# Opening of a chunked-attention and two-MLP kernel: planned with shared DMA time, block 1's attention right behind block 0's, sixteen weight halves' low parts summed on TensorE

## Chip, cores and metric

One core of a Trainium2 chip. The metric is the device time of one execution in microseconds (us), the median of several runs; a profile of one execution shows where it goes.

## What is computed

```python
# q, k, v: 8 x 8 heads x 576 x 64 float32; attention within chunks of 64
scores = scale * np.matmul(q_c, k_c.transpose(0, 1, 2, 4, 3))
scores = scores - np.max(scores, axis=-1, keepdims=True)
attn = np.exp(scores)
attn = attn / (np.sum(attn, axis=-1, keepdims=True) + 1e-09)
out = np.matmul(attn, v_c)
x = out.transpose(0, 2, 1, 3).reshape(4608, 512)
h = x @ w_in                                  # 512 x 2048, float64 weights
g = np.maximum(h, 0.0) + np.log1p(np.exp(-np.abs(h)))
x2 = (g @ w_out).astype(np.float32)           # 2048 x 512
h2 = np.maximum(np.maximum(x2 @ w1, x2 @ w2), x2 @ w3)   # 512 x 768 each
result = (h2 @ w_out2).astype(np.float32)     # 768 x 512
```

## The kernel before

The 4608 tokens are cut into nine blocks of 512 (`NB`). For each block four attention tiles (two heads each) give x in four buffers, then the first MLP runs over 16 column groups j of the hidden size (`NJ`): `mlp1` computes one group's h (`do_h`, line 712, 12 matmuls of 512 columns into a bank `ph`), ScalarE its softplus, ScalarE and VectorE cut g into a high and a low part, and `do_o` (line 732, 12 matmuls) adds into the accumulator `acc`. Each product is made of three passes over high and low parts (`PASS`) in the format fp32r. The second MLP (lines 880 and 990) follows for all blocks.

Blocks 0 and 1 share the opening. Their order is the list `turns`: block 0 for j 0 to 5, block 1 for j 0 to 8, block 0 for j 6 to 15, block 1 for j 9 to 15; a block whose turn ends early copies its accumulator out to memory and adds it again later. Their eight attention tiles (`attention_first`) use TensorE in plain float32: transposes of k and q (line 495), scores (`do_s`, line 526), a softmax on VectorE and ScalarE, a transpose of it (line 486), the product with v (`do_v`, line 575), and a cut into high and low part (`to_x`). Block 0's tiles take any PSUM buffer; block 1's take only `aps`, of which there is one, and come due in the middle of block 0's first turn.

Each of the 32 weight halves (`conv1`: w_in and w_out of each j) comes from memory as raw float64 (512 KB); VectorE makes of it a float32 value `a` and a rest `t` in six instructions (lines 292 to 320), an engine rounds the high part from `a`, and two more VectorE instructions, in `cut_up`, form the low part (`a` minus the high part, plus the rest; line 251). Lines 244, 246 and 251 are helpers that record all copies and two-operand operations.

The order of instructions on each engine is made ahead of time by a planner (`Plan.order`): a list schedule with due times, costs and latencies written by hand, and buffers given out as it goes. On the chip each engine then runs its list in order and waits on semaphores. DMAs are issued by SyncE (SP), and for the first two blocks by ScalarE too; a DMA waits in its engine's list until the DMA eight before it in the program has landed.

Of the kernel before, what the change touches and what calls it, by code (L numbers as in the profile page):

```python
# [20 lines left out]
P = 128  # L21
# [32 lines left out]
class Op:  # L54
    __slots__ = ("engs", "fn", "deps", "allocs", "bufs", "due", "n", "start", "end", "eng", "lat", "succ", "left", "ready", "follow")


class Plan:
# [6 lines left out]
    def op(self, engs, fn, r=(), w=(), alloc=(), hold=(), after=(), due=None, lat=0.0):  # L65
        o = Op()
        o.follow = o.start = None
        o.engs, o.fn, o.due, o.lat, o.allocs = engs, fn, due, lat, list(alloc)
        deps = dict.fromkeys(after)
        bufs = dict.fromkeys(o.allocs + list(hold))  # L70
        for item in r:
            b, key = item if isinstance(item, tuple) else (item, None)
            deps.update(dict.fromkeys(b.writers[key] if key in b.writers and key is not None else sum(b.writers.values(), [])))
            bufs[b] = None
        for item in w:
            b, key = item if isinstance(item, tuple) else (item, None)
            if key is None:
                deps.update(dict.fromkeys(sum(b.writers.values(), []) + sum(b.readers.values(), [])))
            else:
                deps.update(dict.fromkeys(b.writers.get(key, []) + b.readers.get(key, []) + b.readers.get(None, [])))  # L80
            bufs[b] = None
        for item in r:
            b, key = item if isinstance(item, tuple) else (item, None)
            b.readers.setdefault(key, []).append(o)
        for item in w:
            b, key = item if isinstance(item, tuple) else (item, None)
            b.writers[key] = [o]
        for b in bufs:
            if b.first is None:
                b.first = o  # L90
            else:
                deps[b.first] = None
        o.deps = list(deps)
        o.bufs = list(bufs)
        for b in o.bufs:
            b.uses += 1
        o.n = len(self.ops)
        self.ops.append(o)
        return o

    def order(self):
# [13 lines left out]
        now, done = 0.0, []  # L115
        while len(done) < len(ops):
            taken = []
            virt = dict(engine)
            for o in waiting:
# [26 lines left out]
                o.end = engine[best] + o.lat  # L146
                running.append(o)
# [26 lines left out]
def tile_kernel(ctx: ExitStack, tc: tile.TileContext, q, k, v, w_in, w_out, w1, w2, w3, wo2, out):  # L174
# [82 lines left out]
    turns = [(0, 0, 6), (1, 0, 9), (0, 6, NJ), (1, 9, NJ)]  # L257
# [13 lines left out]
    def conv(src, view, kinds, due=None, after=(), most=("load",)):  # L271
# [4 lines left out]
        def load(e):  # L276
# [8 lines left out]
        in_line("load", op({"S": 0.5}, load, w=[raw], alloc=[free, raw], after=after, lat=4.0))  # L285
# [34 lines left out]
            lambda e: nc.vector.scalar_tensor_tensor(t.t, lw().bitcast(U32), 2.0**-52, t.t, ALU.mult, ALU.mult),  # L320
            r=[raw],
            w=[t],
# [15 lines left out]

    def parts_of(z, *keys):
# [61 lines left out]
    def loads(fns, buf, key, alloc=(), engs="S", after=()):  # L401
        for n, fn in enumerate(fns):
            op(
                {e: 0.48 for e in engs},
                lambda e, fn=fn: fn((nc.scalar if e == "A" else nc.sync).dma_start),
                w=[(buf, (key, n))],
                alloc=alloc if n == 0 else (),
                after=after,
                lat=2.2,
            )  # L410
# [9 lines left out]

    def flat(z):
        return z.t if z.place[0] == "ph" else z.t[:, 0]
# [35 lines left out]
    def attention_first(t, after=()):  # L458
# [14 lines left out]
        slow = 1.7  # L473
# [3 lines left out]
        loads(load_plain(t, q, rq), bq, "q", allocs[0], "SA", after)  # L477
        loads(load_plain(t, k, rk), bk, "k", allocs[1], "SA", after)
        loads(load_v(t, rv), bv, "v", allocs[2], "SA", after)
# [22 lines left out]
        op({"P": 0.44 * slow}, turn_in(pk, rk), r=reads(bk, "k"), w=[pk], alloc=[pk])  # L502
# [8 lines left out]
        op({"P": 0.44 * slow}, turn_in(pq, rq), r=reads(bq, "q"), w=[pq], alloc=[pq])  # L511
# [11 lines left out]
        def do_s(e):  # L523
# [11 lines left out]
            {"P": 1.75 * slow},  # L535
# [24 lines left out]
        o = op({"P": 0.44 * slow}, turn(pp, lambda h: pbuf.t[:, h * P:(h + 1) * P]), r=[pbuf], w=[pp], alloc=[pp], due=due_p)  # L560
# [11 lines left out]
        def do_v(e):  # L572
# [11 lines left out]
            {"P": 1.75 * slow},  # L584
# [8 lines left out]
    def attention(t):  # L593
# [5 lines left out]
        loads(load_32(t, q, lambda: Rq.t), Rq, "q", [Rq])  # L599
        loads(load_32(t, k, lambda: Rk.t), Rk, "k", [Rk])  # L600
        loads(load_v(t, lambda: Rv.t), Rv, "v", [Rv])
# [101 lines left out]
    def mlp1(b, j, first, last):  # L703
# [44 lines left out]
        for m in range(KD) if last else ():  # L748
# [14 lines left out]
            else:  # L763
                copy_op(lambda o=o: o.t, src, [acc[m // 2]], [o], psum=True, alloc=[o], due=T0 + STEP * (s + 4))
            store[b, m] = op(
                {"S": 0.48}, lambda e, o=o, m=m, to=to: nc.sync.dma_start(out=to[b][:, m, :], in_=o.t), r=[o], lat=2.5
# [13 lines left out]
    def early(n, due, after):  # L780

        if n < NJ2:
            a, t, _ = conv(wo2, ("out", n), ("x",), after=after)
            z = slot("x")
            cut_up(z, lambda: a.t, [a], alloc=[z], rest=t, due=due)
            store["o", n] = op({"S": 0.48}, lambda e: nc.sync.dma_start(out=wo2d[n], in_=z.t.bitcast(F32)), r=[z], lat=3.0)
# [4 lines left out]
        store["w", n] = op({"S": 0.48}, lambda e: nc.sync.dma_start(out=w2d[n], in_=a.t), r=[a], lat=2.5)  # L791

    def weights2(n):
# [4 lines left out]
        for h, z in enumerate((a, b)):  # L798
# [6 lines left out]
                lat=2.5,  # L805
# [14 lines left out]
    def split(b, after):  # L820
        names = ("B11", "T1", "T2", "B21", "T3", "T4", "B22")
        raw = [slot("x", "z", dt=F32) for _ in range(2)]
        for h in range(2):
# [6 lines left out]
                lat=4.0,  # L830
# [139 lines left out]
    def mlp2_out(b, j):  # L970
# [9 lines left out]
                lat=3.5,  # L980
# [59 lines left out]
    op({"G": 1.0}, lambda e: make_identity(nc, ident), due=-10.0)  # L1040
# [5 lines left out]
    for t in range(HP):  # L1046
        attention_first(t)
    for j in range(NJ):
        c0 = T0 + STEP * (min(place[b, j] for b in range(2)) - 1.5)
        conv1(("a", j, 0), w_in, ("in", j), c0)  # L1050
        done = conv1(("a", j, 1), w_out, ("out", j), c0 + 0.5 * STEP)
        for t in range(HP, 2 * HP) if j == 1 else ():
            attention_first(t, [line["load"]])
    store_early = []
    for n, (b, j, first, last) in enumerate(steps):
        if n >= NJ and n % (NJ // HP) == 0:
            t = HP + n // (NJ // HP)
            if t < NTILE:
# [3 lines left out]
                attention(t)  # L1062
# [46 lines left out]
```

## Time and profile before

| | us |
|---|---|
| median of 3 runs | 1579.29 (1577.02 to 1582.55) |
| the profiled execution | 1575.96 |
| its span, first to last instruction | 1573.8 |
| TensorE busy in it | 1516.1 (96%) |
| VectorE busy | 969.7 (62%) |
| ScalarE busy | 584.5 (37%) |

The profiled execution's own time is 2.2 us above its span. Shares of busy time are averages over stages that differ: the opening, with attention, weight conversion and first loads, and the long rest, in which TensorE alone works without a pause. "The join" is used below for the moment when TensorE starts the first `do_h` of block 1: from then on both blocks have all their attention behind them.

### The profile page before, as it was taken

To read this page: it belongs to the slowest core of one execution; us is meant where nothing else is said; L and a number is where in the kernel's file an instruction comes from. 1 tells how busy PE (TensorE), PEld (TensorE's weight loads), DVE (VectorE), ACT (ScalarE), POOL (GpSimd) and SP (SyncE) were. 2 spreads that over 40 slices of the span, in tenths; PEclk is the share of its full clock that TensorE was granted. 3 is DMA by queue.
4 is the path that set the end of the run, shared out by engine and by line. 5 is a ranking of instruction groups with operands and counts; after the bars stand their busy time and mean duration, and the time that the engine had idled before them with its cause. 6 is when DMAs were issued, how large, how long until landed. Compare 5 with 4: busy or idle time off the path is not lost.

```text
span 1573.8 us, 22841 instructions
## 1 busy us (share of the span) xinstructions
PE 1516.1 (96%) x8866; PEld 1315.8 (84%) x8866; DVE 969.7 (62%) x1859; ACT 584.5 (37%) x1111; POOL 11.9 (1%) x19
## 2 busy tenths in 40 slices
PE   5687999999999999999999999999999999999998
PEld 4566888788888888888888888999999999999997
DVE  4798887786776676776857455544544535445443
ACT  3554244443433434334343343433323323223222
POOL 2000010000000000000000000000000000000000
PEclk8798999999999999999999999999999999999999
DMA  9423314453433434335333121222213223222221
GB/s 248 120 81 103 105 40 112 123 132 98 121 97 75 117 86 108 81 72 132 84 96 102 61 95 54 68 81 81 85 63 108 81 68 108 80 82 73 76 81 67
DMA packets 235211, 147.26 MB, mean 94 GB/s; under 512 B 167008, under 2 KB 202848, under 8 KB 235104
## 3 DMA queue, kind: packets, MB, share of 16 engines
q1 hardware_dynamic: 230544, 143.58, 32.2%
q10 hardware_dynamic: 4560, 2.23, 0.6%
q8 instruction: 69, 1.13, 0.3%
q14 instruction: 38, 0.31, 0.1%
HBM read 109.58 MB, written 36.18 MB: 93 GB/s over the span
## 4 chain that ended last, share of the span: by engine, by line
PE 90%; DVE 4%; DMA 2%; ACT 1%; SPq 1%; issue 1%; ACTq 0%; DVEq 0%
PE acc L732 25%; PE ph L712 25%; PE ph L880 12%; PE aps L880 12%; PE acc L990 10%; DVE tmp L251 3%; PE aps L689 3%; PE aps L636 2%; PE aps L575 1%; ACT s L244 1%; DMA s<-in_v_dram 1%; DMA s<-in_k_dram 1%; PE aps L495 1%; DVE s L251 1%; DMA s<-in_q_dram 0%
## 5 line engine op out<-in xcount | busy, mean ns | idle before, releaser
L732 PE MATMUL acc<-g,s 128*128 128x512 f32 x1728 | 429.1, 397 | 2.3 <-DVE g L251 2.3
L712 PE MATMUL ph<-s,s 128*128 128x512 f32 x1728 | 419.0, 392 | 0.9 <-DVE s L251 0.8
L732 PEld LDWEIGHTS acc<-g,s 128*128 128x128 f32 x1728 | 322.7, 188 | 78.2 <-DVE g L251 2.8
L712 PEld LDWEIGHTS ph<-s,s 128*128 128x128 f32 x1728 | 321.9, 188 | 72.2 <-DVE s L251 1.7
L251 DVE TENSOR_TENSOR tmp<-aps,tmp 128x256 f32<-128x256 f32 x241 | 99.3, 422 | 280.6 <-PE aps L880 217.4
L880 PE MATMUL ph<-s,s 128*128 128x256 f32 x1944 | 267.5, 282 | 0.0
L880 PEld LDWEIGHTS ph<-s,s 128*128 128x128 f32 x1944 | 251.6, 191 | 4.4
L244 ACT COPY tmp<-ph 128x256 f32<-128x256 f32 x268 | 99.8, 372 | 352.9 <-PE ph L880 350.9
L251 DVE TENSOR_TENSOR g<-tmp,g 128x512 fp32r<-128x512 f32 x198 | 134.1, 688 | 134.9 <-ACT g L244 133.5
L880 PE MATMUL aps<-s,s 128*128 128x256 f32 x1458 | 203.7, 285 | 3.6
L722 ACT ACTIVATE tmp<-ph 128x512 f32<-128x512 f32 x144 | 86.3, 599 | 302.9 <-PE ph L712 300.7
L880 PEld LDWEIGHTS aps<-s,s 128*128 128x128 f32 x1458 | 186.1, 191 | 9.0 <-DVE tmp L251 8.6
L990 PE MATMUL acc<-s,g 128*128 128x512 f32 x648 | 160.2, 396 | 1.9 <-ACT g L244 1.9
L244 ACT CAST s<-tmp 128x512 fp32r<-128x512 f32 (+2 forms) x197 | 119.1, 610 | 82.2 <-DVE tmp L607 38.6
L251 DVE TENSOR_TENSOR s<-tmp,s 64x512 fp32r<-64x512 f32 (+1 forms) x212 | 141.6, 674 | 12.4 <-ACT s L244 9.1
L990 PEld LDWEIGHTS acc<-s,g 128*128 128x128 f32 x648 | 118.5, 189 | 27.3 <-ACT g L244 2.2
L244 ACT CAST g<-tmp 128x512 fp32r<-128x512 f32 x187 | 116.2, 621 | 48.6 <-PE acc L732 36.5
L251 DVE TENSOR_TENSOR tmp<-tmp,tmp 128x256 f32<-128x256 f32 (+1 forms) x152 | 82.9, 547 | 3.9
L251 DVE TENSOR_TENSOR s<-aps,s 64x512 fp32r<-64x512 f32 x66 | 45.0, 682 | 12.8 <-ACT s L244 11.6
L244 ACT COPY p<-aps 64x512 f32<-64x512 f32 x38 | 22.1, 583 | 73.5 <-PE aps L636 70.4
L689 PEld LDWEIGHTS aps<-s,s 128*64 128x64 f32 x672 | 44.5, 135 | 5.8 <-DVE s L251 1.2
L689 PE MATMUL aps<-s,s 128*64 128x128 f32 x672 | 45.1, 223 | 1.6 <-DVE s L251 1.1
(81 smaller groups left out, 936.8 us busy)
## 6 DMA issues: line engine op xcount, KB each, us to landing
s<-wo2d SPq DMA_DIRECT2D x54, 512.0 KB, 3.3
s<-in_moe_w_out_dram SPq DMA_DIRECT2D x22, 512.0 KB, 4.5
x2d<-tmp SPq DMA_DIRECT2D x36, 256.0 KB, 2.7
s<-in_moe_w_dram SPq DMA_DIRECT2D x18, 512.0 KB, 4.5
s<-x2d SPq DMA_DIRECT2D x18, 512.0 KB, 5.1
s<-in_moe_w_in_dram SPq DMA_DIRECT2D x16, 512.0 KB, 4.6
out_dram<-tmp SPq DMA_DIRECT2D x29, 256.0 KB, 4.4
pd<-tmp SPq DMA_DIRECT2D x28, 256.0 KB, 2.0
```

What stands on the lines that cost most here:

```text
L244: nc.scalar.copy(dst(), src())
L251: return op({"D": 0.69 * n}, lambda e: nc.vector.tensor_tensor(dst(), a(), b(), f), r=r, w=w, **kw)
L495: nc.tensor.transpose(dst.t[:D, h, g * P:(g + 1) * P], i[:, h, g, :], ident)
L575: nc.tensor.matmul(o[:CH, c], rv()[:, c * CH:(c + 1) * CH], blk[1]()[:, c].rearrange("p e s -> p (e s)"), start=True, stop=True,)
L636: nc.tensor.matmul(o[:, h], Qh.t[:, l, h * P:(h + 1) * P], kb[m].t[:, 2 * h * P:2 * (h + 1) * P], start=(n == 0), stop=(n == 2),)
L689: nc.tensor.matmul(o[:CH, c], Vh.t[:, l, c * CH:(c + 1) * CH], z[m][:, c % 2, c // 4, c // 2 % 2], start=(n == 0), stop=(n == 2),)
L712: nc.tensor.matmul(ph.t, w[:, wi, kk * P:(kk + 1) * P], x[kk].t[:, xi], start=(kk == 0 and wi == 0 and xi == 0), stop=(kk == KD - 1 and wi ...
L722: in_line("y", op({"A": 0.6}, lambda e: nc.scalar.activation(l.t, ph.t, AF.Softplus), r=[ph], w=[l], alloc=[l]))
L732: nc.tensor.matmul(acc[m // 2].t[:, m % 2], w[:, wi, m * P:(m + 1) * P], g.t[:, gi, :], start=(first and wi == 0 and gi == 0), stop=(last ...
L880: nc.tensor.matmul(dst(), ws.t[:, wi, col + kk * P:col + (kk + 1) * P], x.t[:, xi, kk * HT:(kk + 1) * HT], start=(first and kk == 0 and wi ...
L990: nc.tensor.matmul(acc[t // 2].t[:, t % 2], g.t[:, gi, t * P:(t + 1) * P], wo.t[:, wi], start=(j == 0 and wi == 0 and gi == 0), stop=(j == ...
```

## The change

Four edits. The planner gets a second cost of a DMA, `move`: the time that all DMAs need one after the other on shared engines, by which planned landing times and due times move; all loads and stores get such a cost, and costs of the first tiles' TensorE work are set anew. The attention of block 1 gets a due time of 38 us plus 5 us a tile (before, 64 us plus 0.6 us a tile), may use all PSUM buffers, and loads through SP alone; block 0's loads get early due times, and those of block 2 and later wait for a weight load each (`first_loads`). `turns` becomes block 0 for j 0 to 3, block 1 for j 0 to 7, then the rests. And for j 0 to 7, 16 weight halves, the low part is made on TensorE: three matmuls add minus the high part, the value and the rest in a PSUM bank (by an identity and its negative, `eye`), and ScalarE copies the bank out; the two VectorE instructions of `cut_up` are left out.

```diff
-    turns = [(0, 0, 6), (1, 0, 9), (0, 6, NJ), (1, 9, NJ)]
+    SUMS = 8
+    turns = [(0, 0, 4), (1, 0, 8), (0, 4, NJ), (1, 8, NJ)]
...
         for o in reversed(ops):
-            c = min(o.engs.values()) + o.lat + 0.3
+            c = min(o.engs.values()) + max(o.lat, o.move + 1.8 if o.move else 0.0) + 0.3
...
                 o.end = engine[best] + o.lat
+                if o.move:
+
+                    moved = max(moved, now + 1.0) + o.move
+                    o.end = max(o.end, moved + 0.8)
...
-        in_line("load", op({"S": 0.5}, load, w=[raw], alloc=[free, raw], after=after, lat=4.0))
+        in_line("load", op({"S": 0.5}, load, w=[raw], alloc=[free, raw], after=after, lat=2.0, move=2.2))
...
     def conv1(key, src, view, due):
-        a, t, last = conv(src, view, ("z", "w"), most=("load", "load0"))
         w = wbuf[key] = slot("w")
-        cut_up(w, lambda: a.t, [a], alloc=[w], rest=t, due=due)
+        kw = dict(most=("load", "load0"))
+        if key[1] >= SUMS:
+            a, t, last = conv(src, view, ("z", "w"), **kw)
+            cut_up(w, lambda: a.t, [a], alloc=[w], rest=t, due=due)
+            return last
+
+        a, t, last = conv(src, view, ("z", "w"), rest=w, **kw)
+        copy_op(lambda: w.t[:, 0], lambda: a.t, [a], [(w, "h")])
+        ps = Buf("ph", "aps")
+
+        def sums(e):
+            o = flat(ps)
+            nc.tensor.matmul(o, eye.t[:, 1, :P], w.t[:, 0], start=True, stop=False)
+            nc.tensor.matmul(o, ident, a.t, start=False, stop=False)
+            nc.tensor.matmul(o, eye.t[:, 0, :P], w.t[:, 1], start=False, stop=True)
+
+        op({"P": 1.4}, sums, r=[eye, a, (w, "h"), (w, "rest")], w=[ps], alloc=[ps])
+        copy_op(lambda: w.t[:, 1], lambda: flat(ps), [ps], [(w, "l")], psum=True, due=due, engs="A", after=[last])
         return last
...
-        any_ps = ("acc", "aps", "ph") if t < HP else ("aps",)
-        two_ps = ("acc", "aps") if t < HP else ("aps",)
-        due_v = 18.0 + 5.0 * t if t < HP else T0 + STEP * (5.7 + 0.1 * (t - HP))
+        any_ps = ("acc", "aps", "ph")
+        two_ps = ("acc", "aps")
+        due_v = 18.0 + 5.0 * t if t < HP else 38.0 + 5.0 * (t - HP)
...
-        loads(load_plain(t, q, rq), bq, "q", allocs[0], "SA", after)
+        engs = "SA" if t < HP else "S"
+        first = -60.0 + 4.0 * t if t < HP else None
+        loads(load_plain(t, q, rq), bq, "q", 1.1, allocs[0], engs, after, first)
...
-                attention(t)
+                attention(t, [first_loads[min(t, 11)]])
```

The planner moves instructions on every engine. Three places follow, rows of the program's order, each an instruction (or several) with its line, output, inputs and shape.

TensorE between block 0's last scores and its second product with v. Before (`tmp_70`, `tmp_73` are block 0's first two softmax tiles, `s_24_279` block 1's first k and q):

```order
L526 MATMUL acc_88<-s_14_181,s_9_151 128x256 x4
L495 MATMUL aps_87<-ident,s_24_279 64x128 x8
L486 MATMUL acc_89<-ident,tmp_70 128x128 x4
L575 MATMUL acc_88<-s_16_198,s_2_133 64x128 x8
L486 MATMUL acc_89<-ident,tmp_73 128x128 x4
L495 MATMUL aps_87<-ident,s_24_279 64x128 x8
L575 MATMUL acc_89<-s_18_214,s_5_143 64x128 x8
```

Of the change (lines 557, 517 and 606 are 526, 486 and 575 of before; lines 368 to 370 are the sums):

```order
L557 MATMUL acc_88<-s_14_169,s_8_138 128x256 x4
L517 MATMUL acc_89<-ident,tmp_68 128x128 x4
L368 MATMUL ph_85<-s_25_224,s_11_152 128x512
L369 MATMUL ph_85<-tmp_66,ident 128x512
L370 MATMUL ph_85<-s_25_224,s_11_152 128x512
L606 MATMUL acc_89<-s_16_175,s_2_132 64x128 x8
L517 MATMUL acc_88<-ident,tmp_69 128x128 x4
L606 MATMUL acc_88<-s_19_191,s_4_134 64x128 x8
```

Block 1's transposes are no longer between block 0's scores and its softmax transposes; a sum is.

ScalarE while it cuts block 0's x (`s_36_426` and `s_39_472` before, `s_27_348` and later after) into parts. Before, with `rv_77`, a v tile of block 2:

```order
L244 COPY s_28_291<-aps_87 64x512 x2
L244 CAST s_37_461<-tmp_71 128x512
L244 CAST s_38_464<-rv_77 128x512
L244 CAST s_39_472<-acc_89 64x512
L244 COPY s_20_229<-aps_87 64x8x64 x2
L244 COPY s_23_255<-ph_85 64x8x64 x2
```

Of the change:

```order
L249 CAST s_36_386<-ph_86 128x512
L249 COPY s_22_207<-aps_87 64x8x64 x2
L249 COPY s_24_213<-ph_85 64x8x64 x2
L249 CAST s_39_453<-aps_87 64x512 x2
L249 CAST s_38_426<-ph_86 128x512
L249 CAST s_40_457<-ph_85 128x512
```

The cast of block 2's v has gone from here (it stands some 80 rows later), and copies of sums out of PSUM have come.

TensorE just ahead of the join. Before, after six groups of block 0 (line 732 is the last `do_o` of them):

```order
L732 MATMUL acc_89<-g_65,s_59_789 128x512 x6
L732 MATMUL acc_88<-g_65,s_59_789 128x512 x6
L575 MATMUL aps_87<-s_16_198,s_28_291 64x128 x8
L575 MATMUL aps_87<-s_18_214,s_29_293 64x128 x8
L575 MATMUL aps_87<-s_20_229,s_30_295 64x128 x8
L575 MATMUL aps_87<-s_23_255,s_31_298 64x128 x8
L712 MATMUL ph_86<-s_65_962,s_32_300 128x512 x3
```

Of the change (743 is `do_h`, 763 `do_o`; the last row is the join):

```order
L606 MATMUL acc_89<-s_22_207,s_33_357 64x128 x8
L606 MATMUL acc_88<-s_24_213,s_35_359 64x128 x8
L368 MATMUL ph_86<-s_54_752,s_11_152 128x512
L369 MATMUL ph_86<-tmp_67,ident 128x512
L370 MATMUL ph_86<-s_54_752,s_11_152 128x512
L368 MATMUL ph_85<-s_57_801,s_11_152 128x512
L369 MATMUL ph_85<-tmp_66,ident 128x512
L370 MATMUL ph_85<-s_57_801,s_11_152 128x512
L763 MATMUL acc_89<-g_63,s_36_386 128x512 x6
L763 MATMUL acc_88<-g_63,s_36_386 128x512 x6
L743 MATMUL ph_86<-s_53_729,s_25_224 128x512 x3
```

Before, 12 units (a `do_h` or a `do_o`) stand ahead of the join; of the change, five units and ten sums, and the products with v alternate between PSUM buffers.

## Rows read from the trace of the kernel before

**Rows 1.** The page: TensorE busy and its granted clock in 40 slices

```profile
PE   5687999999999999999999999999999999999998
PEclk8798999999999999999999999999999999999999
```

**Rows 2.** Busy us by stretch: PE, weight loads, DVE, ACT, POOL, clock, DMA share, GB/s

```profile
0.00:71.00 71.00, 41.10 (x213) 34.20 (x214) 38.46 (x78) 31.55 (x53) 7.89 (x15) 0.76 0.78 204
71.00:145.00 74.00, 58.46 (x286) 48.40 (x284) 66.98 (x139) 35.04 (x59) 0.00 (x0) 0.91 0.25 79
145.00:300.00 155.00, 154.98 (x750) 127.45 (x750) 123.01 (x230) 62.67 (x108) 4.05 (x4) 1.00 0.35 93
300.00:309.00 9.00, 6.59 (x45) 4.95 (x44) 8.58 (x15) 3.27 (x6) 0.00 (x0) 1.00 0.33 57
309.00:800.00 491.00, 491.00 (x2573) 407.80 (x2572) 347.39 (x618) 199.50 (x340) 0.00 (x0) 1.00 0.40 100
```

**Rows 3.** Waits of TensorE, 0 to 160 us: total, times, longest

```profile
PE aps L495 <- ACT s L244: 11.3, 3, 8.8
PE aps L575 <- DVE s L251: 9.2, 3, 3.9
PE aps L495 <- DMA s<-in_k_dram: 7.5, 2, 6.8
```

**Rows 4.** Timeline of the opening: start, duration, engine, instructions, wait before

```profile
21.75 3.62 PE L526 MATMUL acc<-s,s 128*128 128x256 f32 x16
27.11 1.97 PE L526 MATMUL acc<-s,s 128*128 128x256 f32 x8 [1.74 <-ACT tmp L244]
30.99 0.58 ACT L244 COPY tmp<-acc 64x512 f32<-64x512 f32 x1 [3.28 <-DMA s<-in_v_dram]
35.86 1.89 PE L495 MATMUL aps<-ident,s 128*64 128x128 f32 x8 [6.79 <-DMA s<-in_k_dram]
46.51 1.96 PE L575 MATMUL acc<-s,s 128*64 128x128 f32 x16
48.41 0.66 PE L486 MATMUL aps<-ident,tmp 128*128 128x128 f32 x4
56.05 0.62 ACT L244 CAST s<-rv 128x512 fp32r<-128x512 f32 x1 [7.36 <-DMA rv<-in_v_dram]
68.14 1.06 PE L495 MATMUL aps<-ident,s 128*64 128x128 f32 x8 [0.21 <-DVE s L251]
71.29 8.44 PE L712 MATMUL ph<-s,s 128*128 128x512 f32 x36
```

**Rows 5.** Timeline ahead of the join, TensorE and one VectorE stretch

```profile
129.22 3.68 PE L575 MATMUL aps<-s,s 128*64 128x128 f32 x16 [3.88 <-DVE s L251]
131.41 0.68 DVE L251 TENSOR_TENSOR tmp<-tmp,s 128x512 f32<-128x512 f32 x1
132.01 0.42 DVE L306 TENSOR_SCALAR tmp<-tmp 128x512 int32<-128x512 int32 x1
132.35 0.68 DVE L251 TENSOR_TENSOR s<-tmp,tmp 128x512 fp32r<-128x512 f32 x1
135.57 3.37 PE L575 MATMUL aps<-s,s 128*64 128x128 f32 x16 [2.67 <-DVE s L251]
141.61 3.43 PE L575 MATMUL aps<-s,s 128*64 128x128 f32 x16 [2.67 <-DVE s L251]
144.96 8.94 PE L712 MATMUL ph<-s,s 128*128 128x512 f32 x36
```

**Rows 6.** Timeline of TensorE in the long part: its pace

```profile
318.78 2.91 PE L712 MATMUL ph<-s,s 128*128 128x512 f32 x12
321.53 2.97 PE L732 MATMUL acc<-g,s 128*128 128x512 f32 x12
324.34 1.60 PE L689 MATMUL aps<-s,s 128*64 128x128 f32 x24
```

**Rows 7.** DMA and busy time from 2 to 28 us, columns as in rows 2

```profile
2.00:28.00 26.00, 18.46 (x92) 15.03 (x93) 12.52 (x25) 9.70 (x18) 6.48 (x8) 0.87 1.11 291
```

**Rows 8.** SP's last issues of block 0's v

```profile
13.58 1.28 SPq L394 DMA_DIRECT2D s<-in_v_dram  x2
```

More of the change, by code (lines that the diff above doesn't have):

```diff
@@ L54 @@
 class Op:
-    __slots__ = ("engs", "fn", "deps", "allocs", "bufs", "due", "n", "start", "end", "eng", "lat", "succ", "left", "ready", "follow")
+    __slots__ = ("engs", "fn", "deps", "allocs", "bufs", "due", "n", "start", "end", "eng", "lat", "succ", "left", "ready", "follow", "move")
 class Plan:
@@ L63, in __init__, with op @@
         self.free = {k: list(v) for k, v in places.items()}
-    def op(self, engs, fn, r=(), w=(), alloc=(), hold=(), after=(), due=None, lat=0.0):
+    def op(self, engs, fn, r=(), w=(), alloc=(), hold=(), after=(), due=None, lat=0.0, move=0.0):
         o = Op()
+        o.move = move
         o.follow = o.start = None
@@ L114, in order @@
         running = []
-        now, done = 0.0, []
+        now, done, moved = 0.0, [], 0.0
         while len(done) < len(ops):
@@ L268, in in_line, with conv @@
         return o
-    def conv(src, view, kinds, due=None, after=(), most=("load",)):
+    def conv(src, view, kinds, due=None, after=(), most=("load",), rest=None):
         raw, a, t, free = slot(*kinds, shape=[P, TB, 2], dt=I32), Buf("tmp"), Buf("tmp"), Buf(*most)
@@ L399, in load_v, with loads @@
                 yield fn
-    def loads(fns, buf, key, alloc=(), engs="S", after=()):
+    def loads(fns, buf, key, move, alloc=(), engs="S", after=(), due=None):
+        fns = list(fns)
+        if alloc:
+            op({"S": 0.0}, lambda e: None, alloc=alloc, after=after)
         for n, fn in enumerate(fns):
             op(
-                {e: 0.48 for e in engs},
+                {e: 0.5 for e in engs},
                 lambda e, fn=fn: fn((nc.scalar if e == "A" else nc.sync).dma_start),
                 w=[(buf, (key, n))],
-                alloc=alloc if n == 0 else (),
                 after=after,
-                lat=2.2,
+                lat=1.8,
+                move=move / len(fns),
+                due=due,
             )
@@ L476, in attention_first @@
         blk = [lambda z=z: z.t.rearrange("p (u e s) -> p u e s", e=2, s=CH) for z in s1]
[L477 to L479 removed]
+        engs = "SA" if t < HP else "S"
+        first = -60.0 + 4.0 * t if t < HP else None
+        loads(load_plain(t, q, rq), bq, "q", 1.1, allocs[0], engs, after, first)
+        loads(load_plain(t, k, rk), bk, "k", 1.1, allocs[1], engs, after, first)
+        loads(load_v(t, rv), bv, "v", 1.6, allocs[2], engs, after, first and first + 10.0)
         pq, pk = Buf(*two_ps), Buf(*two_ps)
@@ L591, in attention_first, with attention @@
         to_x(t, pv)
-    def attention(t):
+    def attention(t, after=()):
         due_v = T0 + STEP * (4 * (t - HP) + 2.25)
@@ L979, in mlp2_out @@
                 after=[store["o", j], *begun],
[L980 removed]
+                lat=2.0,
+                move=2.2,
             ),
@@ L1039, in tile_kernel @@
     op({"G": 0.1}, lambda e: nc.gpsimd.memset(drop, -DROP), due=-11.0)
-    op({"G": 1.0}, lambda e: make_identity(nc, ident), due=-10.0)
+    made = op({"G": 1.0}, lambda e: make_identity(nc, ident), due=-10.0)
+    eye = slot("vh")
+    for n, f in enumerate((1.0, -1.0)):
+        op(
+            {"D": 0.2},
+            lambda e, n=n, f=f: nc.vector.tensor_scalar(eye.t[:, n, :P], ident, f, None, ALU.mult),
+            w=[(eye, n)],
+            alloc=[] if n else [eye],
+            after=[made],
+            due=-9.0,
+        )
     def zeros(name, after):
```

44 lines of the change are left out of this document (25 added, 19 removed).

## Prediction

> **What bounds the kernel now.** I read the page's slices first, to see where TensorE is not busy. After the first tenth of the span it is at 9 in every slice but the last [rows 1]: almost all that is to be won lies in the opening. The table by stretch says how much. From 145 us on TensorE works through: 154.98 of 155 us, then a hole of 2.4 us around 302 to 308 us, then 491 of 491 [rows 2]. The opening is two stages. Up to 71 us (block 0's first `do_h` starts at 71.29 [rows 4]) TensorE is busy 41.1 of 71 us and VectorE 38.5: neither is the limit, they wait in turn. From 71 to 145 us VectorE is busy 67.0 of 74 us and TensorE 58.5 [rows 2]: there the conversions of weights, block 1's softmax and its cutting of x queue on VectorE.
>
> The waits and the timeline name the pieces. In the first stage the longest are TensorE's 6.79 us at 29 us, for block 1's k, whose transposes stand in front of block 0's softmax transposes, and 7.36 us in which ScalarE sits in front of a cast of block 2's v that has not been loaded, while TensorE waits 8.8 us for the copies behind it [rows 3, 4]. In the second stage block 1's four products with v go through the single buffer `aps`, so each waits for the cut of the one before: three start 6.0 to 6.4 us apart although the product itself takes 3.4 to 3.7 us (and would take 2.0, as at 46.51) [rows 4, 5]. The join comes at 144.96 us [rows 5].
>
> **The change, part by part.** Since TensorE has no holes to speak of behind the join, the end moves by what the join moves, corrected for work moved past it.
>
> *Work moved past the join.* Seven units fewer stand ahead of it. A unit's pace is (324.34 - 318.78)/2 = 2.78 us [rows 6], so 19.5 us of work comes later. Ten of the 16 sums stand ahead of the join and six behind. The trace has no sum; its pieces have near rows. Two passes are fp32r of 512 columns, 2.78/12 = 0.23 us each. The middle one is plain float32: the scores' 8 matmuls of 256 columns (16 instructions in the trace) took 3.62 us [rows 4], so 0.45 for 256 columns and 0.90 for 512. A sum is 1.37 us (between 0.7, if the float32 pass ran like the others, and 2.5 at the low clock, below); I take 1.37, since the near row is the same kind of matmul. Sixteen are 21.9 us of new work on the engine that bounds the whole, six of them, 8.2 us, behind the join. So the change breaks even with a join at 144.96 - 19.5 - 8.2 = 117.3 us.
>
> *Up to block 0's first `do_h`.* The two waits go: of the order, block 1's transposes now stand after block 0's last softmax transpose, and the cast of block 2's v is far behind. They lie one after the other, so both count: 6.8 + 7.4 = 14.2 us. (ScalarE's 3.28 us behind its own DMA issues at 27 to 31 us [rows 4] lies inside the first, so it is not counted.) The loads: the queues moved 291 GB/s from 2 to 28 us [rows 7], and block 0's last v is issued only at 13.58 us, because weight halves stand between [rows 8]. Now block 0's 3.15 MB (four tiles, q, k and v of 256 KB each) and one weight half, 0.5 MB, go first: 3.67 MB at 291 GB/s is landed near 14.6 us, about when the last v was only being issued. Against that, the half in front delays the first k. I take 5 us for an earlier last score (bounds 0 and 7). Five sums come ahead, 6.9 us; TensorE has 30 us of holes there [rows 2], so between nothing and all of it counts, and I take half. 71.3 - 14.2 - 5 + 3.4 = 55.5 us, between 52 and 64; say 56. VectorE's list up to there is not shorter (77 instructions before, 78 after), so it is covered by holes as before: 38.5 busy of 71.
>
> *From there to the join.* TensorE's list: 5 units, 13.9 us; 5 sums, 6.9; 4 groups of transposes at 1.06; 3 scores at 1.81; 4 softmax transposes at 0.66; 4 products with v at 1.96 [rows 4]: 40.9 us. VectorE's list: 72 instructions, of which some 21 short ones follow each other at 0.34 us and 43 long ones at 0.60 (132.01 to 132.35, 131.41 to 132.01 [rows 5]), 8 tiny: 34 us. It was 67. Two things took that away: each conversion with a sum leaves out two long instructions, 1.2 us, 19.2 us over all 16, and conversions for later j are no longer due before the join. ScalarE gets a copy of 0.58 us for each (the copies' price at 30.99 [rows 4]) and has room: 35 of 74 busy. So TensorE's list is now the longer, and with several PSUM buffers the products need not wait for each other's cut; what is late next is the chain score, softmax, transpose, product of each tile. Without a hole the stage takes 41 us; at the density of before, 58.5 of 74, 52. I take 85%, 48 us. Join: 56 + 48 = 104 us, between 93 and 116.
>
> *The clock.* The price of TensorE's work is not fixed: the same group of eight transposes took 1.89 us right after the 6.79 us of idle and 1.06 at 68.14 [rows 4], and the mean granted clock was 0.76 of 2.4 GHz up to 71 us, 0.91 then, and 1.00 behind the join [rows 2], so the lower level, 1.2 GHz, held for half of the first stage. The Trainium skill (TensorE: Matmul & The Clock Gate, Part 1: The HAM clock gate) says that the low rate is the default, that it returns after idleness, and that sustained activity releases it. By that rule the change's holes decide the price of its sums: ten at the low level would be 10 x 1.37 x 1.89/1.06 = 24.4 us instead of 13.7, and the join 11 us later. The row agrees that this happens after a wait; whether the new order has such waits no row shows. My first stage has before's clock in it, the second takes full speed.
>
> *The hole near 305 us.* It stands where block 2 needs its last attention tile. In the new order that tile's product comes nine units behind its scores instead of six; I count 1 us of the 2.4.
>
> *Sum.* 117.3 - 104 = 13.3 us, and 1: 14 us off the profiled execution's 1575.96, 1562. This execution is 3.3 us under the median of the runs, 1579.29; against the median the forecast is 1565 us.
>
> **Rivals.** The measurement tells 0.3%, 4.7 us, from no change.
>
> *VectorE is behind at the join.* Block 0's accumulators are handed over after its fourth group, and of the new order ScalarE's copies of them, and of a sum that the next `do_h` but one needs the bank of, stand behind casts that wait for VectorE's conversions 35 instructions past its last cut of x: 21 x 0.34 + 14 x 0.60 = 15.5 us. TensorE gets there 7 units and 2 sums after the join, 22 us. So 6.7 us of lateness are free and each us beyond is lost; with VectorE as packed as before (67 of 74) some 10 us could go. Against it: 34 us of work in 48. Gain 0 to 4, about 1577 us.
>
> *The clock stays low.* If the second stage has the 0.76 of the first, its 41 us become 54, at 85% 63, and the join comes at 119: 1580 us. For it: each sum stands in TensorE's list between steps that wait for other engines. Against: from 71 us on, with holes of a fifth, the clock was 0.91 [rows 2]. It is what the Trainium skill's rule (TensorE: Matmul & The Clock Gate, Part 1) would give if the new order keeps the long waits.
>
> *The sums hold up TensorE (slower).* TensorE runs its list in order. A sum waits for its half's six VectorE instructions, 4 x 0.34 + 2 x 0.60 = 2.6 us, and a cast of 0.62; if the half is always just late, block 1's attention behind it waits too, up to 3.2 us for each of ten sums. At 1.3 us on average the gain is gone, at 1.8 it is slower by 0.3%, at 3.2 the join is at 136 and the time 1597 us. For it: VectorE's list takes the rest of one half only a few instructions ahead of its sum, and the loads come eight at a time. Against: in the first stage VectorE has holes of 32 us, and the sums stand where TensorE would wait for a softmax anyway.
>
> **Chances.** The forecast, with a gain of 5 to 26 us: 0.74; more than that, 0.02; VectorE behind, 0.08; clock low, 0.05, both within 0.3%; sums in the way, slower by over 0.3%, 0.11. So 0.76 faster, 0.13 same, 0.11 slower. Range: the early join, 93, with the whole hole gone is a gain of 26, 1553 us; the late end takes in most of the cases with a gain near nothing, 1577.
>
> **What would show it.** Right: no wait of TensorE for block 1's k and none of ScalarE for `rv` ahead of block 0's first `do_h`; that `do_h` at 52 to 60 us; the join at 95 to 115; the float32 pass of a sum near 0.9 us; VectorE well under 90% from there to the join; TensorE without holes for the 60 us behind it. Wrong: a join later than 117, waits in front of the sums (line 368), or new holes between the join and 300 us, where block 2's attention, planned for a time that has moved, is then late.

## The result, and the profile after

| | before | after |
|---|---|---|
| median, us | 1578.7 (1577.02 to 1582.55, 4 runs) | 1553.23 (1551.45 to 1554.74, 4 runs) |
| profiled execution; its span | 1575.96; 1573.8 | 1553.11; 1551.4 |
| TensorE busy; idle in the span | 1516.1; 57.7 | 1524.7; 26.7 |
| first `do_h` of block 0; the join | 71.29; 144.96 | 56.28; 95.13 |

The ratio is 0.9835, 95% interval 0.9814 to 0.9856: 25.5 us faster, where the prediction had 14 and a range of 1553 to 1577. The direction holds, the size does not: the time lies at the fast end of the range. TensorE is busy 8.6 us more (the sums, less what attention became cheaper, below) and idle 31 us less.

The page after, TensorE and its granted clock in 40 slices; only the first slice and, as before, the last are below 9 now (beside [rows 1]):

```profile
PE   6999999999999999999999999999999999999998
PEclk9999999999999999999999999999999999999999
```

The stretches of after (columns as in [rows 2]), cut at the first `do_h` and at the join; the first row is all that lies ahead of the join, the second a short piece that the last section speaks of:

```profile
0.00:95.13 95.13, 79.57 (x452) 63.33 (x453) 81.92 (x157) 60.48 (x104) 7.88 (x15) 1.00 0.63 169
12.00:16.00 4.00, 3.11 (x15) 2.55 (x16) 2.49 (x4) 1.61 (x4) 0.00 (x0) 1.00 1.36 187
0.00:56.00 56.00, 40.44 (x233) 31.70 (x234) 46.05 (x82) 31.20 (x54) 7.88 (x15) 1.00 0.91 244
56.28:95.13 38.85, 38.85 (x219) 31.34 (x217) 35.59 (x76) 29.00 (x51) 0.00 (x0) 1.00 0.22 61
145.00:300.00 155.00, 153.78 (x786) 126.97 (x785) 120.35 (x221) 65.82 (x111) 3.82 (x4) 1.00 0.37 98
300.00:309.00 9.00, 9.00 (x40) 7.29 (x39) 8.38 (x18) 4.14 (x8) 0.00 (x0) 1.00 0.38 102
```

The same stretch ahead of the join before:

```profile
0.00:144.96 144.96, 99.52 (x496) 82.56 (x496) 105.40 (x216) 66.59 (x112) 7.89 (x15) 0.84 0.51 140
```

From `do_h` to the join TensorE works 38.85 of 38.85 us. Ahead of the join it was idle for 45.4 us before and for 15.6 after, so the join, 49.8 us earlier, is made of 29.9 us of idle time, 19.5 of units moved past it and 0.5 of the rest, in which ten sums (13.8 us) came in and the eight attention tiles became 14.3 us cheaper (99.52 less 12 units, 66.2; 79.57 less 5 units and 10 sums, 51.9): after the first 20 us their instructions have the price of the higher clock now. The timeline shows both prices:

```profile
12.89 1.91 PE L526 MATMUL acc<-ident,s 128*64 128x128 f32 x8 [3.72 <-DVE s L251]
20.19 1.04 PE L526 MATMUL acc<-ident,s 128*64 128x128 f32 x8
56.28 3.01 PE L743 MATMUL ph<-s,s 128*128 128x512 f32 x12
76.02 0.48 PE L368 MATMUL ph<-s,s 128*128 128x512 f32 x1
76.34 1.02 PE L369 MATMUL ph<-tmp,ident 128*128 128x512 f32 x2
76.79 0.79 PE L370 MATMUL ph<-s,s 128*128 128x512 f32 x1
77.42 2.92 PE L743 MATMUL ph<-s,s 128*128 128x512 f32 x12
80.28 1.96 PE L606 MATMUL acc<-s,s 128*64 128x128 f32 x16
82.17 0.66 PE L517 MATMUL acc<-ident,tmp 128*128 128x128 f32 x4
82.58 2.99 PE L743 MATMUL ph<-s,s 128*128 128x512 f32 x12
85.42 0.60 PE L517 MATMUL acc<-ident,tmp 128*128 128x128 f32 x4
85.94 3.71 PE L606 MATMUL acc<-s,s 128*64 128x128 f32 x32
89.58 0.50 PE L368 MATMUL ph<-s,s 128*128 128x512 f32 x1
91.00 0.40 PE L368 MATMUL ph<-s,s 128*128 128x512 f32 x1
92.33 2.96 PE L763 MATMUL acc<-g,s 128*128 128x512 f32 x12
95.13 2.92 PE L743 MATMUL ph<-s,s 128*128 128x512 f32 x12
```

A sum is 1.42 us (89.58 to 91.00) or 1.33 (91.00 to 92.33), and two products with v follow each other at 1.86 us each (85.94, x32) where they stood 6.0 to 6.4 us apart [rows 5]. After the first 15 us TensorE waits little in the opening: 6.3 us from there to the first `do_h`. The longest of its waits from 0 to 320 us follow, columns as in [rows 3]. "Issue" means that the profile shows nothing that the engine waited for. There is no wait for block 1's k, and ScalarE has none for block 2's v, whose cast comes at 139.48 us. The last row, 0.9 us at 284 us, with another wait of 0.3 us just ahead of it, stands where the program has the hole that lay near 305 us before:

```profile
PE acc L526 <- DMA s<-in_q_dram: 5.6, 1, 5.6
PE acc L526 <- DVE s L251: 3.7, 1, 3.7
PE acc L606 <- issue: 2.6, 1, 2.6
PE ph L368 <- ACT s L249: 1.2, 1, 1.2
PE ph L743 <- DVE s L256: 0.9, 1, 0.9
```

### The profile page after: what moved, and what is told of

Same layout as the page of the kernel before. It is cut to its first block, busy times and chain, and to the rows that moved or that the text cites. A ratio compares the mean times of both kernels' runs of the same rounds, so it can differ in the third digit from the quotient of the medians.

```text
span 1551.4 us, 23011 instructions
## 1 busy us (share of the span) xinstructions
PE 1524.7 (98%) x8930; PEld 1318.1 (85%) x8930; DVE 963.3 (62%) x1834; ACT 594.9 (38%) x1122; POOL 11.7 (1%) x19
## 4 chain that ended last, share of the span: by engine, by line
PE 94%; DVE 4%; DMA 1%; ACT 0%; issue 0%; ACTq 0%; DVEq 0%
PE acc L763 26%; PE ph L743 25%; PE ph L913 13%; PE aps L913 12%; PE acc L1024 10%; DVE tmp L256 3%; PE aps L720 3%; PE aps L667 3%; DMA s<-in_q_dram 1%; PE acc L557 1%; PE acc L606 1%; PE ph L369 1%; PE acc L526 0%; ACT s L249 0%; DVE s L256 0%
## 5 line engine op out<-in xcount | busy, mean ns | idle before, releaser
L913 PEld LDWEIGHTS aps<-s,s 128*128 128x128 f32 x1458 | 186.0, 191 | 9.0 <-DVE tmp L256 8.8
L249 ACT CAST s<-tmp 128x512 fp32r<-128x512 f32 (+2 forms) x190 | 115.1, 609 | 67.4 <-DVE tmp L638 26.6
L249 ACT COPY p<-aps 64x512 f32<-64x512 f32 x50 | 29.1, 582 | 68.8 <-PE aps L667 52.8
L249 ACT COPY tmp<-acc 128x512 f32<-128x512 f32 (+1 forms) x66 | 37.3, 588 | 34.2 <-PE acc L1024 17.0
L667 PEld LDWEIGHTS aps<-s,s 128*128 128x128 f32 x336 | 43.8, 189 | 2.6
```

The costliest lines, as they stand in the source:

```text
L249: nc.scalar.copy(dst(), src())
L667: nc.tensor.matmul(o[:, h], Qh.t[:, l, h * P:(h + 1) * P], kb[m].t[:, 2 * h * P:2 * (h + 1) * P], start=(n == 0), stop=(n == 2),)
L913: nc.tensor.matmul(dst(), ws.t[:, wi, col + kk * P:col + (kk + 1) * P], x.t[:, xi, kk * HT:(kk + 1) * HT], start=(first and kk == 0 and wi ...
```

## The experiments

"A" and "B" are each run's own theories, a rival counted as B. Medians are of 4 to 6 runs; those of before, on the chips on which the four groups of experiments ran, were 1578.52, 1579.8, 1579.84 and 1579.47 us (9 to 11 runs).

### One part of the change undone

**Without sums.**

```diff
-    SUMS = 8
+    SUMS = 0
```

> The changed kernel with SUMS = 0: all 32 low parts are made by VectorE again, the rest of the change stays. Five units and no sum stand ahead of the join; 21.9 us of TensorE work are gone. Theory A (the holes of 71 to 145 us came from block 1's chain through one PSUM buffer): few holes come back, at most 10 us, so the sums are a loss and the time is 1533 to 1545 us, join at 82 to 92 us. Rival B (VectorE was the limit and the sums relieve it): VectorE's list to the join grows by 12 us or more, holes of TensorE come back for 20 us or more, join at 95 to 110 us, time 1551 to 1565 us.

Measured: 1559.39 us (ratio 0.9879, 0.9864 to 0.9894), first `do_h` at 56.73, join at 93.45. The time is B's, and 6.2 us above the change although 22 us of TensorE's work are gone; the join lies between A's and B's. The stage from `do_h` to the join took 36.72 us; behind the join TensorE waits for VectorE (its stretches, and then the waits from 145 to 320 us):

```profile
56.73:93.45 36.72, 33.07 (x200) 27.62 (x198) 35.38 (x73) 27.22 (x48) 0.00 (x0) 1.00 0.10 33
145.00:200.00 55.00, 51.53 (x212) 41.23 (x210) 48.18 (x99) 19.49 (x34) 0.95 (x1) 0.94 0.31 101
200.00:300.00 100.00, 90.95 (x480) 75.42 (x479) 78.36 (x138) 41.67 (x71) 3.07 (x3) 0.97 0.42 101
```

```profile
PE acc L763 <- DVE g L256: 5.4, 2, 3.5
PE aps L667 <- DVE s L256: 4.3, 2, 2.8
PE aps L667 <- DVE s L251: 2.8, 1, 2.8
```

So most of TensorE's new idle time lies behind the join, 12.5 us of holes there (3.5 and 9.0), where the change has 1.2. What of it VectorE's relief takes away, and what the sums themselves fill, the last two runs tell apart.

**Block 1's attention in one buffer again.**

```diff
-        any_ps = ("acc", "aps", "ph")
-        two_ps = ("acc", "aps")
+        any_ps = ("acc", "aps", "ph") if t < HP else ("aps",)
+        two_ps = ("acc", "aps") if t < HP else ("aps",)
```

> The changed kernel, but block 1's attention may use only the buffer aps again; due times, turns, loads and sums as changed. Eight units and all 16 sums now stand ahead of the join, so without new holes it would come at 95.1 + 3 x 2.78 + 6 x 1.37 = 111.7 us and the time be 1553 us. Theory A: the products with v again follow each other at some 6 us, holes of 8 us or more, join at 120 to 130 us, time 1561 to 1572 us. Rival B: no more than 3 us of holes, 1553 to 1557 us.

Measured: 1561.39 us (0.989, 0.9877 to 0.9904), 8.2 us above the change: A; first `do_h` at 50.97, the join at 120.84 with 8 units and all 16 sums ahead of it. With the change's density the same work would have put the join at 95.13 + 3 x 2.78 + 6 x 1.38 = 111.7. The stage is busy 62.59 of 69.87 us, and it lost most of it after 100 us, where the last softmax transposes and products with v take turns in `aps` and wait for the copies and cuts that free it; the products start 4.7 to 6.8 us apart again (stretch, then timeline):

```profile
100.00:145.00 45.00, 38.30 (x184) 29.23 (x183) 39.60 (x82) 21.74 (x38) 0.00 (x0) 1.00 0.34 106
```

```profile
107.49 1.96 PE L606 MATMUL aps<-s,s 128*64 128x128 f32 x16 [1.28 <-ACT s L249]
114.24 1.96 PE L606 MATMUL aps<-s,s 128*64 128x128 f32 x16 [1.47 <-DVE s L251]
118.95 1.96 PE L606 MATMUL aps<-s,s 128*64 128x128 f32 x16 [1.23 <-DVE s L256]
```

**Without the planner's cost of a DMA.**

```diff
-        o.move = move
+        o.move = 0.0
```

> The changed kernel, but the planner takes no shared DMA time into account (the move cost of every DMA is zero); loads keep their new due times, engines and order of release, and the same units and sums stand ahead of the join. If the planner's DMA cost is what makes the order fit the arrivals, the first do_h of block 0 comes some 4 to 10 us after 56.3 us and the time is 1557 to 1565 us; if only the due times, PSUM buffers and sums count, it is 1551 to 1556 us.

Measured: 1552.64 us (0.9836, 0.9821 to 0.985), `do_h` at 56.34, join at 93.80: the second of the two cases expected. This edit alone brings nothing that can be measured.

**All of the loads' part undone.**

```diff
-        o.move = move
+        o.move = 0.0
...
-        engs = "SA" if t < HP else "S"
-        first = -60.0 + 4.0 * t if t < HP else None
+        engs = "SA"
+        first = None
...
-                attention(t, [first_loads[min(t, 11)]])
+                attention(t)
```

> The change with the loads' part undone: no early due times for block 0's loads, block 1's through SP and ScalarE, no wait of later attention loads on weight loads, no planner's cost of a DMA; buffers, due times, turns and all 16 sums as in the change (5 units and 9 sums ahead of the join). Theory A (without sums this part brought 3.8 us at the first do_h and 4.1 us in all, 1563.5 against 1559.4, beside the 9.7 us of the later loads; it adds to the rest): 1560 to 1568. Theory B (the sums fill the waits it leaves, and the planner, with its other edits, has moved the waiting instructions away): 1552 to 1557.

Measured: 1552.72 us (0.9839, 0.9821 to 0.9857), `do_h` at 56.70, join at 92.48 (one sum fewer ahead). B: beside the other parts the new loads bring nothing.

### One part put on the kernel before

**The sums alone** (`conv1`, `conv` and `eye` as in the change, all else before).

```diff
+    SUMS = 8
...
+        op({"P": 1.4}, sums, r=[eye, a, (w, "h"), (w, "rest")], w=[ps], alloc=[ps])
```

> The kernel before, with the 16 sums as its only change: block 1's attention through aps, old due times, turns and DMA planning. 12 units and all 16 sums stand ahead of the join, 21.9 us of new TensorE work in the opening, 19.2 us of VectorE's taken out. Theory A: the waits of the first stage stay and block 1's chain through one buffer still sets the second, so the sums fill holes at best: 1574 to 1590 us. Rival B: with VectorE relieved (67 of 74 us before, about 50 now) the second stage shrinks by 10 us or more: 1560 to 1572 us.

Measured: 1572.77 us (0.9964, 0.9951 to 0.9976), 5.8 us less, between the two ranges. `do_h` came at 60.14 and the join at 138.23. The cast of block 2's v, at 56.05 us before [rows 4], comes at 123.59 here: the planner put it off when the conversions changed.

**The later loads alone.**

```diff
-    def attention(t):
+    def attention(t, after=()):
...
-                attention(t)
+                attention(t, [first_loads[min(t, 11)]])
```

> The kernel before, with one edit: the attention loads of block 2 and later wait for a weight load each, as in the change; with it the cast of block 2's v leaves its place among block 0's copies on ScalarE (the 7.36 us wait there). Block 1's k transposes stay where they are. Theory A (a wait in the first stage counts in full, as the prediction's sum had it): first do_h of block 0 near 64 instead of 71.3, join near 137.5, time 7 us less, 1568 to 1574. Theory B (stage two is held by VectorE and by the one PSUM buffer, and takes back what the first stage gains): first do_h near 64, join 142 to 145, time within 3 us of before.

Measured: 1570.07 us (0.994, 0.9927 to 0.9953), 9.7 us less. A in time. The profiled execution can't be set against that of before piece by piece: at 1573.79 it was the slowest of six, and that of before is under its median. In it `do_h` is at 65.91, near what both had, and the join at 141.51, four us later than A's.

**Buffers, due times and turns alone.**

```diff
-    turns = [(0, 0, 6), (1, 0, 9), (0, 6, NJ), (1, 9, NJ)]
+    turns = [(0, 0, 4), (1, 0, 8), (0, 4, NJ), (1, 8, NJ)]
...
-        any_ps = ("acc", "aps", "ph") if t < HP else ("aps",)
-        two_ps = ("acc", "aps") if t < HP else ("aps",)
-        due_v = 18.0 + 5.0 * t if t < HP else T0 + STEP * (5.7 + 0.1 * (t - HP))
+        any_ps = ("acc", "aps", "ph")
+        two_ps = ("acc", "aps")
+        due_v = 18.0 + 5.0 * t if t < HP else 38.0 + 5.0 * (t - HP)
```

> The kernel before, with block 1's attention in all PSUM buffers, due at 38 us plus 5 us a tile, and the new turns (5 units and no sum ahead of the join); loads, their order and the weight conversions as before. Theory A (holes of stage two come from the one buffer alone; stage two is dense once it is gone, whatever VectorE has to do): first do_h near 71, stage two 34 us of TensorE's list at 90% or more, join 105 to 110, against a break-even of 125.5: gain 15 to 20 less what comes behind the join, 1560 to 1567. Theory B (VectorE, 67 of 74 us busy before, holds stage two when no sum relieves it): join 112 to 122 or holes of 6 us or more within 60 us of the join, time 1568 to 1577.

Measured: 1573.2 us (0.9957, 0.9945 to 0.9969): B in time, but the join is A's, 108.60, and the holes come later than B had them. ScalarE's wait for the v tile (its timeline, first) now falls on TensorE as one wait (waits of TensorE, 0 to 71 us), and the 16.9 us won at the join (125.5 - 108.6) are mostly lost between 200 and 300 us (the stretch, last):

```profile
57.34 0.62 ACT L244 CAST s<-rv 128x512 fp32r<-128x512 f32 x1 [10.57 <-DMA rv<-in_v_dram]
```

```profile
PE acc L575 <- ACT s L244: 12.8, 1, 12.8
```

```profile
200.00:300.00 100.00, 86.86 (x437) 71.27 (x436) 81.38 (x147) 39.92 (x67) 4.02 (x4) 0.95 0.34 83
```

**Both together.** The edits of the last two runs.

```diff
+        two_ps = ("acc", "aps")
...
+                attention(t, [first_loads[min(t, 11)]])
```

> The run before this one and the later loads of block 2's attention together (5 units, no sum ahead of the join). It differs from the change without sums only in the planner's cost of a DMA, the early due times of block 0's loads and SP alone for block 1's. Theory A (the parts add up): first do_h near 64, and the time 5 to 7 us under that run's. Theory B (VectorE is the limit without sums, so an earlier first stage is lost in holes behind the join): join 5 to 7 us earlier, time within 3 us of that run's. The change without sums had its first do_h at 56.7 and 1559.4 us; what is left between is the order of block 0's loads, forecast 5 us.

Measured: 1563.45 us (0.9893, 0.9878 to 0.9908), 16.4 us less, as much as the two apart (9.7 + 6.6). `do_h` 60.51, join 100.02. A, with more than it had: 9.8 us under the run before, and `do_h` 3.5 us ahead of its 64.

### The number of sums

```diff
-    SUMS = 8
+    SUMS = 12
```

> The change with 24 halves summed on TensorE instead of 16 (j 0 to 11); 5 units and 10 sums ahead of the join, as in the change. Theory A (with 16 sums VectorE is no longer late anywhere but 1 us near 200 us, so more sums only add TensorE work): 8 x 1.37 = 11 us more, 1562 to 1566. Theory B (VectorE still holds TensorE up and more relief pays, as the first 16 did): 1548 to 1556.

> The change with 12 halves summed on TensorE instead of 16 (j 0 to 5): ahead of the join nothing differs (5 units, 10 sums), behind it 2 sums instead of 6. Theory A (a sum ahead of the join lies in holes and costs next to nothing, one behind it costs its whole 1.4 us unless VectorE would be late without it): four sums less behind the join, 5.6 us, of which VectorE's lateness gives some back: 1548 to 1551. Theory B (the sums behind the join are needed to keep VectorE in time until 300 us, since without any sum TensorE had 12.8 us of holes there): holes of 4 us or more between 145 and 320 us, 1552 to 1557.

 (`SUMS = 6`)

> The change with 8 halves summed (j 0 to 3): 8 units and 8 sums ahead of the join. Theory A (the first eight sums, which lie in the opening's holes, bring all of the gain of 6.2 us): break-even join 144.96 - 4 x 2.78 = 133.8, and 1545 to 1550. Theory B (relief of VectorE counts by the number of sums: half of the relief, half of the 6.2 us): 1554 to 1558.

 (`SUMS = 4`)

> The change with 12 sums and without the planner's cost of a DMA. That cost alone, taken away, gave 1552.6 against 1553.2, no difference. Theory A: as the run with 12 sums, within 2 us. Theory B (the two orders differ in which sums stand where, and one leaves VectorE late): 3 us or more apart, with holes between 145 and 320 us in the later one.

 (`SUMS = 6` and `o.move = 0.0`)

Measured, with TensorE's idle time from 145 to 320 us:

| sums | 0 | 8 | 12 | 16 | 24 |
|---|---|---|---|---|---|
| us | 1559.39 | 1559.21 | 1554.4 | 1553.23 | 1564.91 |
| idle, 145 to 320 us | 12.8 | 11.8 | 6.2 | 1.2 | 2.0 |

For 24 sums A holds: 8 more cost 11.7 us, 1.46 each, and the idle time that they could have filled was 1.2 us. For 12 it was B, with the holes that it had, though 12 and 16 sums can't be told apart by their times. For 8 neither was right: 1559.21 us is 1.2 over B's range, and no better than without any sum. With fewer sums than 16 TensorE waits between 145 and 320 us, mostly for VectorE. The stretch with 12 sums, and under it with 8:

```profile
145.00:320.00 175.00, 168.85 (x847) 139.12 (x846) 138.04 (x254) 73.75 (x125) 4.37 (x4) 0.99 0.39 103
```

```profile
145.00:320.00 175.00, 163.17 (x797) 133.78 (x796) 141.20 (x263) 69.34 (x118) 4.03 (x4) 0.96 0.38 99
```

12 sums without the planner's DMA cost took 1555.18 us, 0.8 apart: A.

### Price and relief of a sum, taken apart

**Relief alone**: the 16 sums and their copies are left out, so the low part of these halves is only the rest; the due time of the copy goes to the conversion's last step and to the rounding of the high part (not in the diff).

```diff
-        op({"P": 1.4}, sums, r=[eye, a, (w, "h"), (w, "rest")], w=[ps], alloc=[ps])
-        copy_op(lambda: w.t[:, 1], lambda: flat(ps), [ps], [(w, "l")], psum=True, due=due, engs="A", after=[last])
```

> The change with the 16 sums and their copies left out and nothing in their place: the low part of those halves is only the rest (so the value minus the high part is missing from the output). VectorE is relieved as in the change, TensorE does not pay. 5 units and no sum ahead of the join. Theory A (the ten sums ahead of the join lie in holes of the chain; only the six behind it are on the path): join 92 to 95, and 8 us faster than the change for the six sums behind, 1543 to 1548. Theory B (relief makes the chain itself dense, and the sums then stand on the path): second stage 32 to 34 us, join 84 to 90, 16 to 22 us faster than the change, 1531 to 1537.

**Price alone**: VectorE makes all low parts, and the 16 sums are made besides, for nobody; each sum waits for the finished low part, has a due time of its own, and ScalarE does not copy it out.

```diff
-        a, t, last = conv(src, view, ("z", "w"), rest=w, **kw)
-        copy_op(lambda: w.t[:, 0], lambda: a.t, [a], [(w, "h")])
+        a, t, last = conv(src, view, ("z", "w"), **kw)
+        cut_up(w, lambda: a.t, [a], alloc=[w], rest=t, due=due)
...
-        op({"P": 1.4}, sums, r=[eye, a, (w, "h"), (w, "rest")], w=[ps], alloc=[ps])
-        copy_op(lambda: w.t[:, 1], lambda: flat(ps), [ps], [(w, "l")], psum=True, due=due, engs="A", after=[last])
+        op({"P": 1.4}, sums, r=[eye, a, w], w=[ps], alloc=[ps], due=due)
```

> The change with all low parts made on VectorE, as without sums, and the 16 sums made in addition, into a bank that nothing reads. TensorE pays, VectorE is not relieved. 5 units and 8 sums ahead of the join. Theory A (sums ahead of the join lie in holes): join within 3 us of the 93.5 of the run without sums, and the time 5 to 12 us above its 1559.4 (the eight sums behind the join, 11 us, less what falls into the holes that VectorE's lateness leaves there), 1564 to 1572. Theory B (each sum is on the path): join 103 to 106, 1575 to 1582.

Measured (ratios 0.9796, 0.9783 to 0.9809, and 0.9926, 0.9912 to 0.9939; below the first row all is of the profiled executions, "neither" is the run without sums):

| | neither | relief alone | price alone | both (the change) |
|---|---|---|---|---|
| us | 1559.39 | 1547.62 | 1567.28 | 1553.23 |
| first `do_h` | 56.73 | 53.52 | 59.82 | 56.28 |
| `do_h` to the join | 36.72 | 35.97 | 38.49 | 38.85 |
| join | 93.45 | 89.49 | 98.31 | 95.13 |
| sums ahead of the join | 0 | 0 | 8 | 10 |
| idle, 145 to 320 us | 12.8 | 7.1 | 7.7 | 1.2 |
| join to the end of the span | 1464.3 | 1457.1 | 1467.2 | 1456.3 |

The stage from `do_h` to the join and the stretch behind it, relief alone and then price alone:

```profile
53.52:89.49 35.97, 33.21 (x199) 27.56 (x197) 32.54 (x67) 26.76 (x47) 0.00 (x0) 1.00 0.14 45
145.00:320.00 175.00, 167.87 (x858) 138.53 (x857) 140.57 (x259) 73.62 (x126) 4.03 (x4) 0.98 0.40 103
```

```profile
59.82:98.31 38.49, 35.79 (x199) 28.04 (x197) 34.77 (x71) 24.28 (x42) 0.00 (x0) 1.00 0.05 14
145.00:320.00 175.00, 167.35 (x831) 137.22 (x830) 140.27 (x262) 69.51 (x119) 4.04 (x4) 0.97 0.38 101
```

Both times lie in A's ranges: 22 us of sums cost 5.6 us where VectorE is relieved and 7.9 where it is not, and the relief is worth 11.8 to 14.1.

But with relief A's number came out by luck, for A had the price in the wrong place. The ten sums ahead of the join, 13.8 us, cost 5.6 us there (89.49 to 95.13). The six behind it, 8.3 us, cost nothing: TensorE's idle time falls from 7.1 to 1.2 us, and the way from the join to the end is no longer (1457.1 and 1456.3 us). Without relief, eight sums ahead of the join move it by 4.9 us, to 98.31, between A's and B's joins, and eight behind it cost 3.0. So both kinds of holes take in sums, those of the opening and those that VectorE leaves behind the join, and of the 12.8 us idle without sums the relief alone takes away only 5.7.

The join with relief alone is B's, 89.49, but not for B's reason: the stage is hardly shorter (36.0), and the rest is 3.2 us of an earlier `do_h`. The stage takes 36 to 39 us in all four, with no, four or five sums in it. Without sums TensorE is idle there for 3.7 or 2.8 us, with five of them it never is. That it is the chain of block 1's tiles that leaves this idle time is argued from the order; no run tried it by itself.

## Why the prediction was right in direction and wrong in size

*The step that failed: "I take 85%, 48 us"* for the stage from the first `do_h` to the join. The mechanism was right and this term too large. The stage took 38.85 us, so the join came 8.9 us ahead of the 104 forecast, of the 11.8 by which the forecast is too slow. The 85% stood for 7 us in which TensorE would wait between the steps of block 1's chain; it waited for none, busy 38.85 of 38.85 us. The other 2 us are the list, 40.9 us forecast: the durations that it adds up overlap with the next row, as of a softmax transpose that takes 0.66 us while the next instruction starts after 0.41 (82.17 and 82.58). The density of before had been taken over from an order with little else between the steps of its chain. In the new order the stage is busy 90% without sums (33.07 of 36.72 us) and 92% with relief alone; five sums, 6.9 us, then lengthened it by only 2.1 or 2.9 us and left no hole. That the several PSUM buffers are needed for it is shown by the run with one buffer.

*The other 3 us: "3.3 us under the median"*, added to the forecast. It is before's own. Of eleven executions of before the two slowest, 1583.25 and 1581.76 us, had a mean granted clock of 0.980 and 0.979, the two fastest, 1577.18 and 1577.3, 0.984 and 0.986; those of the change were at 0.995 to 0.999 and spread 3.3 us. So the slowest executions had the lowest clock. The profiled execution of after stands at its median (1553.11, 1553.23), so the offset was not to be carried over. That it is the waiting opening which varies, and which the change removes, fits this but is not shown.

*The first `do_h`*: 56 forecast, 56.28 measured, but by luck: two errors cancel. Waits and loads gave 14.6 us (71.29 to 56.73, without sums), where 14.2 + 5 stood. Four or five sums cost 2.8 to 3.1 us there; 3.4 was forecast for five. The relief of VectorE gave 3.2 to 3.5 us, and the prediction counted none. Which edit brings the 14.6 us is not unique: what costs is the cast of block 2's v among block 0's copies, and the later loads, the sums, or the new due times with the sums each make the planner move it (at 56.05 us before [rows 4]; at 107.42, 123.59 and 138.13 in those runs). So the loads' part is worth 13.8 us in kernels without sums (1573.2 to 1559.39; they differ in some planner costs too) and nothing with them (1552.72, 1553.23).

*The price of a sum*: 1.37 forecast, 1.33 to 1.42 measured. The float32 pass, 0.9 forecast, ends 0.86 us after the pass ahead of it (76.02 + 0.48; 76.34 + 1.02).

*VectorE "well under 90%"* to the join was wrong: 35.59 of 38.85 us, 92%, mostly since the stage is shorter (34 us were forecast). TensorE did not wait for it there, with sums and units between the steps of the chain.

*The rival "VectorE is behind at the join"* names what happens without the sums: 12.5 us of holes without any, 6.2 with 12, and 7.1 with the relief alone. It comes 50 us and more behind the join, at block 2's attention and the cutting of g, not at the hand-over of the accumulators. With 16 sums 1.2 us are left. The clause "without holes for the 60 us behind it" held (60.00 of 60 us) and was too weak to tell these kernels apart: the run without sums has that too.

*The rival "the sums hold up TensorE"* did not come: in the whole opening one wait stands in front of a sum, 1.2 us (L368 in the waits of after).

*The clock*: the rival of a low clock did not come; the granted clock was 1.00 in both stages (what the last section says of the first 16 us aside). It did follow the holes: 0.76 in [rows 2] with 30 us of holes, 0.95 from 200 to 300 us in the kernel with 13 us of them. The Trainium skill (TensorE: Matmul & The Clock Gate, Part 1: The HAM clock gate) says that activity releases the low rate and idleness brings it back, and these rows agree. It was a gain that the sum had only for the second stage: attention became 14.3 us cheaper.

*The hole near 305 us*: 1 us of its 2.4 was to go; 1.2 us are left of it, at 282 to 284 us, so right.

No kernel that computes all of it beats the change by more than the measurement can tell; the two with other loads or without the planner's DMA cost (1552.7, 1552.6) are the same. Left open is why relief brings the first `do_h` 3 us forward: which wait goes was not tried by itself.

## What to carry to other kernels

Work moved to the engine that bounds the whole is not to be priced at its length where that engine waits in a chain: price the stage by its chain first, then ask what fits into the holes. Here 22 us of work cost 5.6 us and bought 11.8 of relief; eight sums more, past the last hole, cost their full 1.46 us each. Where in the kernel the price is paid is read from the trace: a total that comes out right can hide two wrong halves. A share of busy time taken over from another order belongs to the chain that made it, and extra independent work raises it.

Where a planner orders everything, parts of a change that remove the same wait don't add: test each part on the kernel before and each taken from the kernel after.

## What was not expected of the hardware

In the first 16 us the record of the granted clock and the durations part: eight transposes at 12.89 us took 1.91 us, as at the low clock before (1.89 at 35.86 [rows 4]), while the granted clock of 12 to 16 us reads 1.00; the same eight took 1.04 at 20.19 (the first rows of the timeline of after, and the second of its stretches). So in the opening the price is read from the duration of an instruction, not from that column.
